# A feed-forward's first product by seven block products, with d_ff passed in two halves

## The chip, the core and the metric

The kernel runs on one core of one Trainium2 chip. The metric is the time of one execution on the device, in microseconds (us). Before the change it is 640.53 us, the median of three runs (640.45 to 642.44).

A core has TensorE (PE, matrix products into PSUM), VectorE (DVE), ScalarE (ACT), GpSimd (POOL), and SyncE (SP), whose queue here issues all transfers between memory and the on-chip buffers.

## The reference

Attention for 4 batches, 8 heads, 768 positions and 64 columns per head, then a feed-forward block on its output. Cut to what matters:

```python
k_sum = k.reshape(B, H, nb, 32, D).max(axis=3)     # nb = 24 blocks of 32 positions
v_sum = v.reshape(B, H, nb, 32, D).mean(axis=3)
scores_l = where(|i - j| < 16, scale * q @ k.T, -1e9)
scores_s = scale * q @ k_sum.T + log(32)
a = softmax(concatenate([scores_l, scores_s]))
x = a @ concatenate([v, v_sum])                    # 3072 tokens of 512 columns
h = x @ w_in                                       # 512 x 2048
g = maximum(h, 0) + log1p(exp(-abs(h)))            # softplus
out = g @ w_out                                    # 2048 x 512
```

The weights come as float64, the rest as float32.

## The kernel before

**Groups and phases.** The 3072 tokens are 12 chunks of 256, three to a batch. Chunks are joined into groups of tokens (line 301): [0, 1], [2], [3, 4], [5, 6], [7, 8], [9, 10], [11]; five hold 512 tokens and two hold 256. The 2048 columns of d_ff are 16 tiles f of 128. The phases (lines 303 and 304) are: group 0 with f 0 to 10, group 1 with f 0 to 10, then both with f 11 to 15, then each further group with all 16. The attention of a group must be done before its phase; it is spread over the phases ahead.

**Attention of a unit** (`attention`, line 557; two heads' pairs of one chunk). TensorE makes scores `sc` (L582), VectorE scales and masks them and takes maxima (L595), ScalarE takes exponentials (L603), VectorE inverts the sums, POOL or VectorE normalizes (L616), VectorE transposes 32x32 squares (L642), which go through memory to finish the transposition (L650, L654), and TensorE multiplies by the value windows (`xo`, L673). The first group uses TensorE for the transposition instead. The block means of v and maxima of k are made once per batch (`Sums`); for the first batch v's come from six matmuls over six loads of 128 positions (`declare_first_values`, L403).

**Precision.** Each operand a of the feed-forward is split into a rounded part and the remainder, ah + al, and each product is three matmuls: ah*bh, ah*bl, al*bh. ScalarE makes `xh` from `xo` (L689), VectorE makes `xl` (L693).

**Weights** (`weights`, line 702). Each tile f is one 512 KB load from w_in (L722) and one from w_out (L719) as 64-bit words. Integer work on VectorE (L735 to L750), ScalarE (L756) and POOL (L764) turns them into two float32 parts (L768, L775). All 16 tiles stay on the chip.

**Feed-forward** (`feed_forward`, line 785). For each f: the first product goes into `ph`, 128 x 512 fp32, in 12 matmuls (L804: four blocks of d_model by three terms); ScalarE takes softplus twice, rounded into `gh` (L824) and exact in place (L828); VectorE takes the difference `gl` (L832); 12 matmuls of the second product add into four `po` tiles (L841). PSUM has eight buffers of 2 KB per partition: four `po`, two for `sc`, and two that `ph` and `xo` share in turn.

```python
ph()[:, :n_x], lhsT=w1()[:, i1, part, cc * P:(cc + 1) * P], rhs=a()[:, cc, :n_x],
start=cc == 0 and i == 0, stop=cc == NCC - 1 and i == 2,
```

**The order of work.** Every piece of work is a task with an engine (or a choice of engines), a declared cost, and the buffers it reads and writes. Tasks are numbered in the order in which the program declares them. The text `SEQUENCE` lists these numbers; a letter takes the second or third choice of engine. `Order.issue` (line 122) runs the tasks' code in that order, so it is the order of each engine's queue, and also the order in which two uses of one buffer follow each other. Engines run their queues in order and wait for each other by semaphores.

Of the kernel before, what the change touches and what calls it, by code (L numbers as in the profile page):

```python
# [75 lines left out]
class Order:  # L76
# [45 lines left out]
    def issue(self, sequence):  # L122

        begun = set()
        for word in sequence.split():
            task = self.tasks[int(word.rstrip("ab"))]
            assert all(other in begun for other, _ in task.after) and task not in begun
            begun.add(task)
            task.ways[" ab".index(word[-1]) if word[-1] in "ab" else 0].run()
        assert len(begun) == len(self.tasks)  # L130
# [17 lines left out]
0 2 64 3 43 4 45 5 68 6 133 7 160 8 51 1 9 47 132 10 44 11 49 12 13 46 14 55 15 72 96 53 16 134a 138a 17 73 151  # L148
161a 74 162 100 84 135 163 142 164 136 137 57 18 165 85 139 19 59 20 166 52 48 86 61 75 76a 65 388 50 70 77 167
21 396a 168 104 66 78 140a 156 141a 147 79 105 69 54 189 143a 56 152a 144 87 58 106 190 153 88a 60 62 145 154  # L150
146 22 116 63 155 80 71 107 157 23 117 24 67 25 26 97 27 148 158 28 169 29 118 30 170 31 108a 32 101 33 34 98 35
149a 99 36 159 37 38 103 39 150 40 102 119 191a 120a 81 179 195 192 89 91 193 90 180 41 92 194 82 93 128 171a 83
196 130 42 94 109 131 111 95 110 199 112 172 309 391 175 173 129 174 197 200 113 389 176 392 121 114 387 123 122
115 390 124 397 198 177 125 178 318 126 181a 219 127 220 185 182 239 310 183 240 201a 184 319 311 202 186 399
312 320 414 313 269 205 325 209 203 187 204 413 321 188 225 416 314 415 326 206 322 315 417 327 400 316 210 221a
317 270 323 207a 208 229 401 324 222 331 223 230 224 289 245 402 403a 329 241a 328 226 422a 332 404 337 405 242
227 279 243 249 333 228 330 338 339 425 244 395 211a 335 334 246 340 215 343 212 235 406 213 247 214 336 344 248
341 426 216 584 345 393 342 250 601 347 346 427 602 217a 604 407 218 348 585 588 349 394 398 231a 408 428 409
290 232 355 350 603 233 234 351 589 236 353 356 352 357 586 605 358 410 429a 237 354 418 255 238 280 359 419
610a 430 420 251a 423 361 587a 431 259 295 252 590 421 253 613 362 254 360 614 256 363 432 365 411 434 424 412  # L160
615 433 257a 367 258 364 594 435 591a 373 368 616 598 617 299 366 369 374 370 371 375 595a 436 376 592 627 599a
372 437 606 628 377 629 380 438 381 378 439 382 593 383 271 631 379 440 441 445 285 442 272 451 273 446 275 274
443 447 596 452 600 444 630 448 276 453 612 449 454 618 260 457 300 619 277a 463 608 458 597 278a 459 450 464
460 455 636a 465 466 456 384 261 461 385 462 265 262 386 469 263 264 639 470 471 472 475 266 654 640 620 611 481
476 477 607 305 478 609 467 291 655 658a 653 468 482 267a 473 483 641 292 474 293 479 484 480 294 487 268 493
296 488 661 485 489 676 494 490 623 495 486 642 622 297 643a 491 621 675 281a 499 496 298a 677 644 492 508 680a
282 500 283 284 501 497 509 502 286 510 498 662 301a 516 511 287a 663 288 683 512 302 804 645 503 303 805 513
304 807 517 806 504 803 664 522 306 505a 812a 506a 518 507 519 665a 307 514 528 666 523 308a 524 525 667 684 515
534 542 529 546 530 685 531 624 815 646 648 520 647 649 686 632 687a 635 521 634 535 688 633 526 637 816 638 536
625 527 689 830 838a 626 817 532 829 537 650 550 668 671 656 533 651 670 551 669 652 538 659 539 543 657 540 552  # L170
818 660 553 541 819a 833 556 831 832 544 548 554 545 557 558 555 559 672 562 673 690 678 674 682 841 563 564 693
# [3 lines left out]
862a 723 865 716 724 725 721 726 860 729 869 881a 866 884 730 731 826 885 722 870 827 834 899 828 886 727 836  # L175
732 901 848 863 728 840 735 850 851 839 887 837 898 741 736 902 835 900 849 737 738 733 742 888a 743 864 734 744
747 907 889 910 748 749 852 750 871 739 877 853 911 890 879 753 854 912 759 891 883 892 754 882 913 914a 740 894
# [3 lines left out]
1042 788 926 793 933 927 794 934 797a 795 798 1043 796 799 928 800a 801 1044 929 935 802 938 930 939 931 940  # L181
1045 1060 941 1046 1047 936 1061 1048 937 1062 942 943 1049 1063 944 1055 1050 1064a 1074 1075 1083a 1051 1077
1065 1076 1078 950 945 1056 1066 1058 946 1059 947 948 951 952 953 1086 956 1087 1067 1068 1069 1088 1070 962
949 957 954 1089 1090a 1091 958 955 963 960 959 1092 964 1100 965 1101 1109a 961 1071 968 1072 1079 1081 1073
1093 1094 1095 1096 974 969 1080 1082 970 1084 971 1085 980 975 1103 1102 976 1104 977 1097 966 1105 1098 1107
1099 1106 1108 1112 981 1110 982 1111 967 1113 1232 972 1236 983 1114 973 978 979 984 1115 1116a 1117 985 986
1233 1118 1237 1234 1238 992 987 1119 1120 988 1121 989 990 993 1122 994 995 998 1235a 1239a 1242 1004 999 1000
1246 1001 1249 1250 1258 1251 1010 1005 1253 1006 1252 1243 991 996 1007 1247 1240 1016 1011 1012 1244 1248 1241
1261 997 1262 1002 1013 1263 1245 1003 1008 1009 1017 1014 1264 1265a 1266 1018 1015 1123 1019 1267 1275 1276
1284 1020 1124 1277 1021 1024 1125 1279 1278 1022 1025 1254 1023 1027 1026 1126 1028a 1268 1269 1270 1271 1029  # L190
1255 1134 1127 1257 1128 1256 1259 1129 1260 1287 1135 1136 1130 1288 1131 1132 1137 1289 1133 1138 1272 1139
1280 1281 1273 1290 1140 1283 1291a 1282 1285 1274 1286 1292 1146 1141 1293 1302 1306 1303 1142 1301 1143 1144
1147 1148 1149 1152 1294 1295 1296 1297 1158 1153 1154 1155 1298 1159 1160 1309 1304 1299 1305 1300 1145 1307
1310 1150 1308 1161 1311 1151 1156 1157 1162 1312 1313a 1163 1314 1164 1315 1324 1328 1325 1323 1170 1165 1316
1166 1317 1167 1168 1318 1171 1319 1172 1173 1176 1320 1177 1178 1331 1326 1321 1179 1327 1322 1169 1329 1332
1174 1330 1333 1175 1180 1181 1182 1334 1335a 1336 1188 1183 1337 1184 1185 1186 1189 1190 1191 1194 1338 1339
# [5 lines left out]
1463 1394 1477 1464 1478 1486a 1401 1480 1479 1465 1481 1399 1400 1402 1407 1466 1467a 1468 1403 1405 1404 1408  # L202
1469 1409 1410 1406 1413 1470 1471 1472 1411 1414 1473 1415 1416 1412 1419 1474 1420 1421 1489 1482 1475 1422
1484 1476 1417 1483 1485 1490 1487 1418 1488 1491 1425 1423 1426 1492 1493a 1424 1431 1494 1427 1428 1495 1429
# [10 lines left out]
def kernel(  # L215
# [731 lines left out]
    for f in range(NF):  # L947
        weights(f)
# [44 lines left out]
```

## Time and profile before

| what | before |
|---|---|
| median of the runs | 640.53 us |
| the profiled execution: its span, first to last instruction | 638.3 us |
| granted clock of TensorE, mean | 0.991 |
| TensorE busy, matmuls | 623.1 us (98%) |
| VectorE / ScalarE / POOL busy | 277.6 / 316.3 / 75.6 us |
| moved by DMA | 86.51 MB, 136 GB/s over the span |
| first product L804 | 960 matmuls of 512 columns and 384 of 256 |
| second product L841 | 1152 matmuls of 512 columns |

The profiled execution's own time is its span and about what lies between that and the median, 2.2 us. Each row of a view names the line, the engine, the operation, what it writes and reads ("gl<-ph,gh"), and a count. "Idle before" is the time that the engine stood before this work, with what ended the wait. In the list of groups a matmul's mean covers its way through the array, and matmuls overlap; what one costs in a stream is read from the chain, where each piece lasts until the next begins.

### The profile page before, as it was taken

What the parts mean: (1) busy time and instruction counts of PE and PEld (TensorE: products, weight loads), DVE (VectorE), ACT (ScalarE), POOL (GpSimd) and SP (SyncE); (2) the same over time, 40 slices, a digit from 0 to 9 for tenths busy, and PEclk for the clock granted to TensorE, in tenths of its full rate; (3) what the DMA queues carried; (4) which work ended last, traced back from release to release, by engine and by line L of the source; (5) the groups of instructions that cost most, each with busy time, mean ns of one, the idle gap of its engine ahead of it and who ended that gap; (6) DMA issues with size and microseconds to landing.
All of it is one profiled execution on the core that took longest, in us unless ns stands there. A gap on an engine that the chain in (4) does not pass through costs nothing.

```text
span 638.3 us, 11177 instructions
## 1 busy us (share of the span) xinstructions
PE 623.1 (98%) x4284; PEld 505.5 (79%) x4284; DVE 277.6 (43%) x753; ACT 316.3 (50%) x762; POOL 75.6 (12%) x70
## 2 busy tenths in 40 slices
PE   7889999999999999999999999999999999999997
PEld 6576777888888888887777877787888888888996
DVE  5879988779643435213451445432411111341111
ACT  4879887479652555215472434462522222552222
POOL 3333322334201130001000030000000000000000
PEclk9889999999999999999999999999999999999999
DMA  9999699744668742141354653453300400311100
GB/s 291 247 262 324 234 224 248 218 139 117 210 201 243 222 139 88 63 134 42 137 167 116 179 143 106 130 145 107 98 1 0 139 1 0 109 57 60 48 1 34
DMA packets 86629, 86.51 MB, mean 136 GB/s; under 512 B 26704, under 2 KB 72368, under 8 KB 86576
## 3 DMA queue, kind: packets, MB, share of 16 engines
q1 hardware_dynamic: 86576, 85.80, 46.2%
q8 instruction: 34, 0.56, 0.3%
q14 instruction: 19, 0.16, 0.1%
HBM read 65.01 MB, written 18.35 MB: 131 GB/s over the span
## 4 chain that ended last, share of the span: by engine, by line
PE 91%; DMA 3%; ACT 3%; SPq 1%; DVE 1%; issue 0%; ACTq 0%
PE po L841 42%; PE ph L804 41%; PE xo L673 4%; PE sc L582 3%; DMA raw<-w_out_dram 2%; DMA k<-kT_dram 1%; ACT sp L603 1%; PE vt L403 1%; DVE sp L616 1%; ACT t L738 0%; SPq L722 0%; ACT pT L633 0%; PE pt L629 0%; ACT raw L756 0%; ACT w L768 0%
## 5 line engine op out<-in xcount | busy, mean ns | idle before, releaser
L804 PE MATMUL ph<-xh,w 128*128 128x512 f32 (+1 forms) x896 | 261.7, 365 | 4.0 <-DVE gl L832 2.5
L841 PE MATMUL po<-w,gh 128*128 128x512 f32 x768 | 204.8, 396 | 0.0
L804 PEld LDWEIGHTS ph<-xh,w 128*128 128x128 f32 x896 | 161.8, 189 | 35.0 <-DVE gl L832 3.1
L832 DVE TENSOR_TENSOR gl<-ph,gh 128x512 fp32r<-128x512 f32 (+1 forms) x112 | 68.2, 611 | 232.5 <-ACT ph L828 211.2
L841 PEld LDWEIGHTS po<-w,gh 128*128 128x128 f32 x768 | 142.3, 188 | 32.7 <-issue 0.8
L804 PE MATMUL ph<-xl,w 128*128 128x512 f32 (+1 forms) x448 | 163.0, 364 | 0.5 <-DVE xl L693 0.5
L824 ACT ACTIVATE gh<-ph 128x512 fp32r<-128x512 f32 (+1 forms) x112 | 60.2, 538 | 207.3 <-PE ph L804 169.3
L841 PE MATMUL po<-w,gl 128*128 128x512 f32 x384 | 115.6, 398 | 0.0
L804 PEld LDWEIGHTS ph<-xl,w 128*128 128x128 f32 x448 | 84.6, 189 | 16.2 <-DVE xl L693 1.3
L841 PEld LDWEIGHTS po<-w,gl 128*128 128x128 f32 x384 | 71.0, 188 | 17.1 <-issue 0.9
L603 ACT ACTIVATE sp<-sp,nm 128x120 f32<-128x120 f32 x192 | 73.1, 382 | 4.4 <-DVE nm L595 4.1
L828 ACT ACTIVATE ph<-ph 128x512 f32<-128x512 f32 (+1 forms) x112 | 59.4, 531 | 0.0
L764 POOL TENSOR_TENSOR t<-t,raw 128x1024 int32<-128x1024 int32 (+1 forms) x18 | 41.8, 2328 | 91.7 <-DVE t L750 26.3
L595 DVE CUSTOM_DVE_ANT_0 sp<-sc,added 128x120 f32<-128x120 f32 x192 | 40.7, 277 | 17.7 <-PE sc L582 17.3
L824 ACT ACT_TABLE_LOAD x24 | 30.8, 1283 | 34.0 <-PE ph L804 30.7
L693 DVE TENSOR_TENSOR xl<-xo,xh 128x512 fp32r<-128x512 f32 x24 | 16.5, 689 | 46.2 <-ACT xh L689 46.2
L603 ACT ACTIVATION_READ_ACCUMULATOR sp<-sp,nm 128x1 f32 x192 | 35.9, 187 | 0.0
L689 ACT CAST xh<-xo 128x512 fp32r<-128x512 f32 x24 | 14.1, 586 | 40.9 <-PE xo L673 40.9
L616 DVE TENSOR_TENSOR sp<-sp,ss 128x960 f32<-128x960 f32 x21 | 26.4, 1258 | 0.5
L673 PEld LDWEIGHTS xo<-pT,v 120*64 120x64 f32 x640 | 20.3, 138 | 7.5 <-issue 6.2
L642 DVE STREAM_TRANSPOSE tb<-sp 128x1024 f32<-128x1024 f32 x20 | 24.8, 1240 | 1.5 <-POOL sp L616 1.2
L353 POOL TENSOR_TENSOR st<-st 96x512 f32<-96x512 f32 (+1 forms) x10 | 10.1, 1011 | 127.9 <-DMA st<-v_hp_dram 127.5
(60 smaller groups left out, 379.4 us busy)
## 6 DMA issues: line engine op xcount, KB each, us to landing
squares<-tb SPq DMA_DIRECT2D x20, 512.0 KB
pT<-squares SPq DMA_DIRECT2D x80, 128.0 KB
raw<-w_in_dram SPq DMA_DIRECT2D x16, 512.0 KB
raw<-w_out_dram SPq DMA_DIRECT2D x16, 512.0 KB
kf<-kT_dram SPq DMA_DIRECT2D x16, 384.0 KB
out_dram<-ob SPq DMA_DIRECT2D x11, 512.0 KB
q<-qT_dram SPq DMA_DIRECT2D x20, 256.0 KB
st<-v_hp_dram SPq DMA_DIRECT2D x12, 384.0 KB
```

Source lines behind the costliest of these rows:

```text
L582: nc.tensor.matmul(unit(g * NU + h * NPAIR + i)[r * QW:(r + 1) * QW, k0:k1], lhsT=q[rows, w * QW:(w + 1) * QW], rhs=k[rows], start=True, s ...
L595: nc.vector.tensor_tensor_reduce(out=sp()[:, n], in0=unit(n), in1=added()[:, kinds.index((lows[w], lows[w + 1]))], scale=-SCALE, scalar=FL ...
L603: nc.scalar.activation(sp()[:, n], sp()[:, n], AF.Exp, bias=nm()[:, n:n + 1], scale=-1.0, accum_out=ss()[:, n:n + 1],)
L616: engine.tensor_tensor(sp(), sp(), s, op=ALU.mult)
L642: nc.vector.transpose(out=tb().rearrange("p k (u q) -> p u k q", q=SQ), in_=tiles.sp().rearrange("p u (k q) -> p u k q", q=SQ),)
L673: nc.tensor.matmul(xo()[h * D:(h + 1) * D, g * CH + w * QW:g * CH + (w + 1) * QW], lhsT=tiles.v(g)[:, w, h * D:(h + 1) * D], rhs=queries(g ...
L764: nc.gpsimd.tensor_tensor(a, a, word(0, I32), op=ALU.add)
L804: nc.tensor.matmul(ph()[:, :n_x], lhsT=w1()[:, i1, part, cc * P:(cc + 1) * P], rhs=a()[:, cc, :n_x], start=cc == 0 and i == 0, stop=cc == ...
L824: nc.scalar.activation(gh()[:, :n_x], ph()[:, :n_x], AF.Softplus)
L828: nc.scalar.activation(ph()[:, :n_x], ph()[:, :n_x], AF.Softplus)
L832: nc.vector.tensor_sub(out=gl()[:, :n_x], in0=ph()[:, :n_x], in1=gh()[:, :n_x].bitcast(F32),)
L841: nc.tensor.matmul(po[t](), lhsT=a()[:, t * P:(t + 1) * P], rhs=w2()[:, i2, part], start=f == f0 and i == 0, stop=f == f1 - 1 and i == 2,)
```

## The change

**Groups and phases.** Six groups of 512 tokens. d_ff is passed in two halves of eight tiles: groups 0 to 4 with the first half, group 5 with all 16, then groups 4, 3, 2, 1, 0 with the second half. The second half's weights are loaded into the buffers of the first half while group 5 is in work (`arrive`). The partial outputs of groups 0 to 4 go to memory and come back, and so does the attention's output x of these groups (`keep`, `attended`). All attention, twenty units after the first four, stands ahead of group 5's phase.

**First product.** For groups 0 and 1 in the first half it stays: 12 matmuls of 512 columns per tile, on xh and xl. Everywhere else two tiles of d_ff are taken together (`hidden_pair`): the product of a 2 x 2 block of weights (128 columns of d_ff and 256 rows of d_model each) with a 2 x 2 block of x (256 rows, 256 tokens) is made of seven block products in place of eight. Each is six matmuls of 256 columns. The products are called by their weight operand: a11, a12, a22 are blocks, s1 to s4 are sums of blocks. They go into halves of two PSUM buffers, `hx` (called z: a11, s2, a12, s4) and `hy` (called y: s3, s1, a22), each of the size of one `ph`, and are combined by a copy p1 and seven VectorE operations of 256 columns: u2, u3, u4 into on-chip buffers, y1, z0, z1, y0 in place. z and y then hold the two tiles. The sums of weights are made once per pair (`sums_of_weights`: joined, combined, and split in two parts), those of x once per group and half (`prepare`: three differences of x blocks more, seven splits in place of four).

**Sums of v.** For the first batch, two loads of 128 positions in place of six; the rest is summed from the value windows that the attention loads anyway, in forty matmuls of 128 columns, one group of ten for each of four pairs of heads.

**Weights.** w_in and w_out are prepared by pairs of tiles, 1024 columns each, w_in by one load of 1 MB; the first pair of each half goes tile by tile.

The numbers of `SEQUENCE` are all new (2346 tasks). In a pair the numbers follow the declarations in `hidden_pair`: with a11 as 2232, p1 is 2233, s3 2234, s2 2235, u2 2236, u3 2237, s1 2238, u4 2239, y1 2240, a12 2241, z0 2242, s4 2243, z1 2244, a22 2245, y0 2246. The lines below hold the first pair of the second half for group 1 (from 2098) and for group 0 (from 2232).

```diff
 SEQUENCE = """
...
+2097a 1941 2048 2053 2056 2057 2218 2049 2061 2058 2062 2072 2063 2088 2068 2098 2099a 2101 2102 2100 2109 2103 2104
...
+2144 2230 2182 2187 2221a 2228a 2185 2148 2190 2191 2149 2183 2189 2192 2222 2168 2071 2231a 2225 2195 2196 2197 2232
+2235 2238 2233 2236 2241 2234 2242 2239 2237 2243 2245 2169 2173 2244 2246 2247 2174 2240 2248 2254 2249 2255 2256
...
-    groups = [[0, 1], [2]] + [[c, c + 1] for c in range(3, len(chunks) - 1, 2)] + [[len(chunks) - 1]]
-    SPLIT = NF // 2
-    phases = [(0, 0, 11), (1, 0, 11), (0, 11, NF), (1, 11, NF)]
-    phases += [(x, 0, NF) for x in range(2, len(groups))]
...
+    groups = [[c, c + 1] for c in range(0, len(chunks), 2)]
+    NX = len(groups)
+    HALF = NF // 2
+    phases = [(x, 0, HALF) for x in range(NX - 1)] + [(NX - 1, 0, NF)]
+    phases += [(x, HALF, NF) for x in reversed(range(NX - 1))]
+    BLOCKS = (0, 1, 2, 3)
+    WHOLE = 2
...
+            parts = {}
+            for i in range(n0, S // P):
+                parts[i] = buffer([P, DM], F32, "vn0", tag="gh", bufs=NU)
...
+            def sum_first(hp, windows, v_keys):
+                def sum_v():
+                    terms = [(ones()[:, NB - 4 * i:2 * NB - 4 * i], part()[:, hp * P:(hp + 1) * P]) for i, part in parts.items()]
+                    for w in range(n0 * P // QW):
+                        rows, of = (KW, shifted) if w else (QW, ones)
+                        terms.append((of()[:rows, NB - 2 * w:2 * NB - 2 * w], windows()[:rows, w]))
+                    for n, (of, values) in enumerate(terms):
+                        nc.tensor.matmul(
+                            total()[KW:KS, hp * P:(hp + 1) * P], lhsT=of, rhs=values,
+                            start=n == 0, stop=n == len(terms) - 1,
+                        )
+                order.add(PE, 2.2, sum_v, [*parts.values(), *v_keys, ones, shifted], [(total, hp)])
...
+        if x:
+            r = block(2 * i + hp // NG)
+            def take(copy):
+                copy(out=r(), in_=xo())
+            order.add(
+                ACT, act(NG * CH, True), lambda: take(nc.scalar.copy), [xo], [r],
+                ways=[Way(DVE, dve(NG * CH), lambda: take(nc.vector.tensor_copy))],
+            )
+            return r
...
+    def keep(x, n, r, held=None):
+        order.add(
+            SP, 0, lambda: nc.sync.dma_start(out=kept(x, n)(), in_=r()), held or [r], [kept(x, n)], size=256 * KiB, row=2048,
+        )
...
+    def prepare(x, n, r):
+        r11, r21, r12, r22 = (r.get(k) for k in range(4))
+        if n == 0:
+            split(r11, *operand(x, 0), NG * CH)
+        elif n == 1:
+            split(r21, *operand(x, 1), NG * CH)
+        elif n == 2:
+            less(r12, r11, r11)
+            split(r11, *operand(x, 2), NG * CH)
+        else:
+            split(r22, *operand(x, 3), NG * CH)
+            less(r22, r12, r12)
+            split(r12, *operand(x, 5), NG * CH)
+            less(r22, r11, r11)
+            split(r11, *operand(x, 4), NG * CH)
+            less(r11, r21, r21)
+            split(r21, *operand(x, 6), NG * CH)
...
+        tiles = [(out_of, i) for i in range(2) for out_of in range(2)] if apart else [(0, None), (1, None)]
+        for outer, which in tiles:
+            fs = [which] if apart else [0, 1]
+            n = len(fs) * DM
+            tag = f"{'wo' if outer else 'wi'}{g}" + (f"_{which}" if apart else "")
...
+                        src = w_in[pair].bitcast(U32)
+                        if apart:
+                            src = w_in[pair, :, :, which * P:(which + 1) * P].bitcast(U32)
...
+        def combined(engine):
+            a11, a12, a21, a22 = (a()[:, i, j] for i in range(2) for j in range(2))
+            engine.tensor_tensor(a22, a21, a22, op=ALU.add)
+            engine.tensor_tensor(a21, a11, a21, op=ALU.subtract)
+            engine.tensor_tensor(a11, a22, a11, op=ALU.subtract)
+            engine.tensor_tensor(a12, a12, a11, op=ALU.subtract)
...
+    TERMS = ((0, 0), (0, 1), (1, 0))
...
+    def hidden_pair(x, f):
+        (w0, of_0), (w1, of_1) = of_w(f), of_w(f + 1)
+        sw = s_bufs[f]
+        y, z = bank([P, 2, CH], "hy"), bank([P, 2, CH], "hx")
+        p1, u2, u3, u4 = (buffer([P, CH], F32, name, bufs=1) for name in ("p1", "u2", "u3", "u4"))
+        def of_s(k):
+            return lambda part, cc: sw()[:, part, k, cc * P:(cc + 1) * P]
+        left = {
+            "a11": (of_0, w0), "a12": (lambda part, cc: of_0(part, NG + cc), w0), "a22": (lambda part, cc: of_1(part, NG + cc), w1),
+            "s2": (of_s(0), sw), "s4": (of_s(1), sw), "s3": (of_s(2), sw), "s1": (of_s(3), sw),
+        }
+        def product(a, n, to, half):
+            lhs, held = left[a]
+            of_x, (buf,) = operand(x, n)
+            def run():
+                y(), z()
+                for cc in range(NG):
+                    for m, (wa, xa) in enumerate(TERMS):
+                        nc.tensor.matmul(
+                            to()[:, half], lhsT=lhs(wa, cc), rhs=of_x(xa)[:, cc * CH:(cc + 1) * CH],
+                            start=cc == 0 and m == 0, stop=cc == NG - 1 and m == 2,
+                        )
+            return order.add(
+                PE, 0.72, run, [(held, 0), (held, 1), (buf, 0), (buf, 1), (y, "whole"), (z, "whole")], [(to, half)],
+            )
+        def combine(out, a, b, op, reads, write):
+            order.add(
+                DVE, dve(CH), lambda: nc.vector.tensor_tensor(out(), a(), b(), op=op), reads, [write],
+            )
+        def half(t, n):
+            return lambda: t()[:, n]
+        begins = product("a11", 0, z, 0)
+        begins.after += [(order.writer[operand(x, n)[1][0], 1], False) for n in range(7)]
+        first_after(begins)
+        order.add(
+            ACT, act(CH, True), lambda: nc.scalar.copy(out=p1(), in_=z()[:, 0]), [(z, 0)], [p1],
+            ways=[Way(DVE, dve(CH), lambda: nc.vector.tensor_copy(out=p1(), in_=z()[:, 0]))],
+        )
+        product("s3", 5, y, 0)
+        product("s2", 4, z, 1)
+        combine(u2, half(z, 1), p1, ALU.add, [(z, 1), p1], u2)
+        combine(u3, half(y, 0), u2, ALU.add, [(y, 0), u2], u3)
+        product("s1", 2, y, 1)
+        combine(u4, half(y, 1), u2, ALU.add, [(y, 1), u2], u4)
+        combine(half(y, 1), half(y, 1), u3, ALU.add, [u3], (y, 1))
+        product("a12", 1, z, 0)
+        combine(half(z, 0), half(z, 0), p1, ALU.add, [p1], (z, 0))
+        product("s4", 3, z, 1)
+        combine(half(z, 1), half(z, 1), u4, ALU.add, [u4], (z, 1))
+        product("a22", 6, y, 0)
+        combine(half(y, 0), u3, half(y, 0), ALU.subtract, [u3], (y, 0))
+        return [z, y]
...
+        pairs = x >= WHOLE or f0 > 0
+            if f0 == 0 and f == HALF:
+                arrive(range(HALF, NF))
+            if not pairs:
+                hs, n = hidden(x, f), 0
+            elif f % 2 == 0:
+                hs, n = hidden_pair(x, f), 0
+            else:
+                n = 1
...
+    def attended(x):
+        r = {}
+        x_bufs.pop(x, None)
+        for n in BLOCKS:
+            order.group = f"a{x}.{n // 2}.{n % 2 * NG}"
+            r[n] = block(n)
+            def load(n=n):
+                nc.sync.dma_start(out=r[n](), in_=kept(x, n)())
+            order.add(SP, 0, load, [kept(x, n)], [r[n]], size=256 * KiB, row=2048)
+            prepare(x, n, r)
+    def arrive(fs):
+        for f in fs[::2]:
+            weights(f // 2)
+        for f in fs[::2]:
+            sums_of_weights(f)
...
+        if x == NX - 1:
+            sums = attend(x, sums)
+        elif x and not f0:
+            sums = attend(x, sums)
+        elif f0:
+            attended(x)
```

More of the change, by code (lines that the diff above doesn't have):

```diff
@@ L485, in load_v @@
                         )
-                    order.add(SP, 0, load_v, [], [self.v_keys[-1]], size=48 * KiB * n, row=512, begin=begin)
+                    order.add(SP, 0, load_v, [], [self.v_keys[-1]], size=48 * KiB * n, row=512)
             def k_sums(copy):
@@ L694, in attention @@
-        order.add(DVE, dve(NG * CH), low, [xo, (xh, c, hp)], [(xl, c, hp)], due=due_x)
-    w_bufs = {}
-    def weights(f):
-        order.group = f"w{f}"
-        for i0, i1 in [(0, 1), (1, 2)] if f < 2 else [(0, 2)]:
-            n = (i1 - i0) * DM
-            tag = f"w{f}_{i0}" if f < 2 else f"w{f}"
+        order.add(PE, 1.2, values, [pT, *((pT, k) for k in range(NSQ)), *tiles.v_keys], [xo])
+        if x:
[7 more added lines that the diff above has]
+            return r
@@ new lines, in attention, with of_x, of_bank, high @@
+        xw = whole_x(x)
+        for g in range(NG):
+            key = xw[hp + g]
+            def of_x(part, key=key):
+                return key[0]()[:, key[1], part, cols]
+            def of_bank(g=g):
+                return xo()[:, g * CH:(g + 1) * CH]
+            def high(of_x=of_x, of_bank=of_bank):
+                nc.scalar.copy(out=of_x(0), in_=of_bank())
+            order.add(ACT, act(CH, True), high, [xo], [(*key, 0, i)])
+            def low(of_x=of_x, of_bank=of_bank):
+                nc.vector.tensor_sub(out=of_x(1), in0=of_bank(), in1=of_x(0).bitcast(F32))
+            order.add(DVE, dve(CH), low, [xo, (*key, 0, i)], [(*key, 1, i)])
@@ L809, in feed_forward @@
-            parts = [range(0, NG), range(NG, NCC)] if x == 0 and f < 2 else [range(NCC)]
-            for ccs in parts:
-                def product_of(ccs=ccs, product=product):
-                    product(ccs)
-                task = order.add(
-                    PE, 0.35 * size * len(ccs), product_of,
-                    [(a, c, hp) for a in (xh, xl) for c in groups[x] for hp in range(0, NHP, NG) if hp in ccs]
-                    + [(w1, i) for i in range(2)],
-                    [ph], due=when, after=[last] if last and ccs[0] == 0 else [],
-                )
-                if ccs[0] == 0:
-                    last = task
@@ L835, in feed_forward @@
-            order.add(DVE, dve(n_x), rest, [ph, gh], [gl])
+            if not pairs:
[4 more added lines that the diff above has]
+                n = 1
+            order.group = f"f{x}.{f}"
+            h = hs[n]
+            halves = [(h, 0), (h, 1)] if pairs else [h]
+            w2, i2, _ = w_out_of[f]
+            gh = buffer([P, CT], F32R, "gh", bufs=4)
+            gl = buffer([P, CT], F32R, "gl", bufs=4)
@@ L837, in project @@
+            order.add(DVE, dve(CT), rest, [*halves, gh], [gl])
             def project(tokens, which, f=f, w2=w2, i2=i2, gh=gh, gl=gl):
@@ L867, in reload @@
                     nc.sync.dma_start(out=ob(), in_=partial[x, i]())
-                order.add(SP, 0, reload, [partial[x, i]], [(ob, 0), (ob, 1)], size=512 * KiB, row=2048, after=[last])
+                order.add(
+                    SP, 0, reload, [partial[x, i]], [(ob, 0), (ob, 1)], size=512 * KiB, row=2048, after=[products[-1]],
+                )
             for t in range(2):
@@ L893, in leave @@
                         nc.sync.dma_start(out=out[r0:r0 + P, :], in_=ob()[:, t])
-                    order.add(SP, 0, leave, [(ob, t)], [], size=256 * KiB, row=2048, due=end + 4)
+                    order.add(SP, 0, leave, [(ob, t)], [], size=256 * KiB, row=2048)
             else:
@@ L947 @@
-    for f in range(NF):
-        weights(f)
+        r = {}
+        for i in range(len(groups[x])):
+            for hp in range(0, NHP, NG):
+                c = groups[x][i]
+                if chunks[c][1] == 0 and hp == 0:
+                    sums = Sums(chunks[c][0])
+                    sums.declare()
+                order.group = f"a{x}.{i}.{hp}"
+                n = 2 * i + hp // NG
+                r[n] = attention(x, i, hp, Places(c, hp, sums, pads), False)
+                if x < NX - 1:
+                    keep(x, n, r[n])
+                if x < WHOLE:
+                    prepare_whole(x, n, r)
+                else:
+                    prepare(x, n, r)
```

524 lines of the change are left out of this document (345 added, 179 removed), and 19 rows, old and new, of the table SEQUENCE.

## The prediction

> **What bounds the kernel now.** I read the page's busy times and slices first, then the time by stages, then the chain that ended last.
>
> ```profile
> span 638.3 us, 11177 instructions
> ...
> PE 623.1 (98%) x4284; PEld 505.5 (79%) x4284; DVE 277.6 (43%) x753; ACT 316.3 (50%) x762; POOL 75.6 (12%) x70
> ...
> PE   7889999999999999999999999999999999999997
> ```
>
> ```profile
> 0.00:100.00 100.00, 88.49 (x814) 68.43 (x818) 79.14 (x192) 78.91 (x173) 32.52 (x39) 0.95 0.94 264
> 100.00:635.00 535.00, 534.65 (x3480) 437.09 (x3472) 198.44 (x562) 237.12 (x590) 43.06 (x31) 1.00 0.38 111
> ```
>
> The columns are PE, PEld, DVE, ACT and POOL, then granted clock, DMA share, GB/s. From 100 us to the last matmul TensorE is busy 534.65 us of 535, at a granted clock of 1.00, with VectorE at 198, ScalarE at 237 and DMA at 0.38. In the first 100 us every resource is crowded: DMA 0.94, VectorE and ScalarE 79, TensorE 88 with waits. So after 100 us a microsecond of matmul removed is a microsecond of span, and a gap put between matmuls is one too. The chain shows the price of a matmul.
>
> ```profile
> 520.54 2.78 PE ph L804 x12
> 523.33 2.78 PE po L841 x12
> ...
> 630.43 1.43 PE ph L804 x12
> 631.87 2.80 PE po L841 x12
> ```
>
> Twelve matmuls of 512 columns take 2.78 to 2.80 us (0.2325 each), and the 256-column ones of the last, half-sized group 1.43 or 1.44 (0.1195 each). A matmul's time goes with its columns, and two halves cost only 2.8% over a whole. That also settles whether the new, narrower products would be held up by their weight loads: the half group loads new weights for each 256-column matmul already.
>
> **The first product.** A pair of hidden tiles took 2 x 2.79 = 5.58 us for 512 tokens. Seven block products of six 256-column matmuls are 42 x 0.1195 = 5.02. Forty pairs go this way (the first two groups keep the plain product for the first half of d_ff): 40 x 0.56 = 22.4 us off. The two half-sized groups disappear as well: 32 products at 1.435 become halves of full ones at 1.395, another 1.3. Together -23.7. The second product and the attention's matmuls stay as they are.
>
> **The sums of v.**
>
> ```profile
> 22.59 4.77 PE vt L403 x10
> ```
>
> Six sums over 512 columns run as twelve instructions of 0.477 us, 5.7 us. Now forty sums of 128 columns run as eighty, at a quarter each 9.5 us: +3.8, all in the start where TensorE waits on others anyway, so between 0 and 3.8; I take 3.8. Four loads of 256 KB go: at the 264 GB/s above 4 us of transfers, which I leave in the bounds of the start below.
>
> **The block products' hand-overs.** This is the term that decides. Each pair writes into two buffers, hx and hy, of 2 x 256 fp32 columns, each the size of one ph. hx takes a11, s2, a12, s4 and hy takes s3, s1, a22. Between them one copy and seven VectorE operations read and rewrite halves of these buffers: p1 and u2 read hx, u3 and u4 read hy, and so on. Before, ph passes as a whole: all matmuls, then all readers, then the next matmuls, with a second ph to hide it. What a passing costs is seen here.
>
> ```profile
> 67.79 0.68 DVE L832 TENSOR_TENSOR gl<-ph,gh 128x512 fp32r<-128x512 f32 x1
> ...
> 68.52 0.50 PE L804 MATMUL ph<-xh,w 128*128 128x512 f32 x1 [1.26 <-DVE gl L832]
> ...
> 68.86 0.39 PE L804 MATMUL ph<-xl,w 128*128 128x512 f32 x1
> ```
>
> ```profile
> 631.58 0.29 PE L804 MATMUL ph<-xh,w 128*128 128x256 f32 x1
> ...
> 631.96 0.39 ACT L824 ACTIVATE gh<-ph 128x256 fp32r<-128x256 f32 x1 [2.16 <-PE ph L804]
> 632.24 0.38 ACT L828 ACTIVATE ph<-ph 128x256 f32<-128x256 f32 x1
> ...
> 632.66 0.42 DVE L832 TENSOR_TENSOR gl<-ph,gh 128x256 fp32r<-128x256 f32 x1 [2.40 <-ACT ph L828]
> ```
>
> The last 256-column matmul starts at 631.58, its slot ends at 631.70, the reader starts at 631.96: 0.26 us. A reader of 256 columns takes 0.39 on ScalarE, 0.42 on VectorE, and one reader follows another after 0.04 (632.62 to 632.66). Back to TensorE: the read ends at 68.47, the matmul starts at 68.52, and its successor is 0.34 later instead of 0.23, so 0.16. A product that must wait for one fresh read of its buffer stands still for 0.26 + 0.42 + 0.16 = 0.84 us, unless a product into the other buffer fills the time.
>
> Does a product into one half wait for a reader of the other half? No row of before shows it, since no buffer there is read while the rest is still being written. The ends are no wait, and the wait for the whole buffer. I take the whole buffer, which is how every ph in the trace changes hands. [...]
>
> I walked the order of words with these prices. The first pair of group 1's second half begins 2098 2099a 2101, which is a11, p1, s2: hx, its reader, hx, with nothing of hy between. It stands bare for 0.84. The first pair of group 0's second half, 2232 2235 2238 2233 2236 2241 2234 2242 2239 2237 2243 2245 is a11, s2, s1, p1, u2, a12, s3, z0, u4, u3, s4, a22. s2 ends at 1.43, p1 (ScalarE) runs 1.69 to 2.08, u2 2.12 to 2.54, a12 may start at 2.70 where s1 ended at 2.15: 0.55. s4 waits 0.13 for z0. s3 ends at 4.13, u4 and u3 end at 5.15, a22 starts at 5.31 against 4.98: 0.33. Sum 1.01 us, against the 0.56 that the pair saves. Over the forty pairs, with the other words of VectorE and ScalarE in their places, it comes to 49 us, from 0.1 to 3.6 a pair (the dear ones have p1 or u2 behind a softplus or a mask). If passing cost nothing and only the readers' own time counted, it would be 26. So 0 to 49, and I take 49: the durations are measured, and only the rule that a half waits for the other is assumed.
>
> The readers themselves, about 3.4 us per pair, fit: VectorE has 337 us free after 100 us, and the forty pairs ask 134.
>
> **The start: when group 1's first product can begin.**
>
> ```profile
> 3.43 7.42 DMA raw<-w_out_dram
> ```
>
> ```profile
> 64.42 2.43 POOL L764 TENSOR_TENSOR t<-t,raw 128x1024 int32<-128x1024 int32 x1 [4.80 <-DVE ss L610]
> ...
> 64.55 3.32 DVE L616 TENSOR_TENSOR sp<-sp,ss 128x960 f32<-128x960 f32 x1
> ```
>
> ```profile
> L616 DVE TENSOR_TENSOR sp<-sp,ss 128x960 f32<-128x960 f32 x21 | 26.4, 1258 | 0.5
> ...
> L750 DVE SCALAR_TENSOR_TENSOR t<-raw,t 128x1024 uint32<-128x1024 uint32 x14 | 17.1, 1225 | 0.4
> ...
> L742 DVE TENSOR_SCALAR t<-t 128x1024 f32<-128x1024 f32 x14 | 10.2, 728 | 2.0 <-ACT t L738 2.0
> L746 DVE TENSOR_SCALAR t<-t 128x1024 uint32<-128x1024 uint32 x14 | 10.1, 722 | 0.5
> ```
>
> Group 1 is now two chunks, and it comes after eight tiles of d_ff instead of eleven, so all its attention stands ahead of it. POOL and VectorE exclude each other here: the multiply that takes 1.258 us on average took 3.32 when it began 0.13 after a POOL add of 2.43. So I add both engines' SBUF work in the words ahead of group 1's first product. POOL: 8,192 columns of weight adds, six normalizations of 960 and about 10,000 columns of low parts and other sums, 24,000 columns at 2.43 per 1,024, 57 us. VectorE: eight times 0.728 + 0.722 + 1.225 = 21 us for the weights' integer steps and, estimated at the same rates, 29 for low parts, casts, magnitudes, normalizations and sums of v, 50 us. The first weights land at 10.85, so 107 us of exclusive work end at 118 at best. Before had done 200 of the two products' matmuls at 100 us; the change needs 192, three more value units (3 us), nearly four more score units (4 us) and the 3.8 above: 109 if TensorE fares as before. So the start loses 9 us. Filled only as VectorE was on average (79 of 100 us) it would end at 146 and lose 37; it loses 0 if work ahead in the order can run later than it stands. I take 12, nearer the low end, as the two engines take turns.
>
> **The rest.**
>
> ```profile
> q1 hardware_dynamic: 86576, 85.80, 46.2%
> ```
>
> ```profile
> SPq L483 <- PE xo L673: 73.5, 15, 10.8
> ```
>
> The x blocks of five groups go to memory and back, and the partial outputs of five groups instead of two: some 18 MB more. At the 111 GB/s for a share of 0.38 that is 62 us of the full DMA, on top of 0.462 x 638 = 295. All attention now comes in the first half; without the second half's weights, the final stores and half of the 18 MB, about 275 us of DMA fall into some 335 us. It is hidden, so 0, but a late load is in the range. The second half's weights are prepared during the last group, with about 94 us of POOL and VectorE work that exclude each other where TensorE has 88 (78 of matmuls, about 10 of hand-overs): between 0 and 15, I take 3. The stores of x wait on SP for their copy, with the next unit's loads queued behind; SP waited 73.5 us in such a place before, for xo, and TensorE lost nothing: 0. The tail stays: four token tiles instead of two, stored one by one.
>
> **Sum.** The profiled span is 638.3, the median of the runs 640.5, so 2.2 lie around it. 640.5 - 23.7 + 3.8 + 12 + 49 + 3 = 684.6, say 685. A measurement of this kernel tells 0.3% (2 us) from no change.
>
> **Rivals.** First, the halves are independent, or the hand-overs are covered: 685 - 49 = 636, and with a start that costs nothing 624. It is the other side: faster from the point where a pair loses less than about 0.1 us, that is 0.56 less the 17.5 us of the other terms over forty pairs. For it: the order names hx and hy by halves in the writes it declares. Against it: ph's whole-buffer turns above. Second, the second half's weights come late and the last group waits for them: +15 in place of 3, 697. For it: 94 against 88. Against it: the loads can begin when the last group leaves each tile. Third, the hand-overs cost the readers' time alone, 26: 662, in the low end of my own range.
>
> **How the numbers follow.** Forecast 0.63 with the third rival in it, own range 655 to 702; first rival 0.25; second 0.12. 630 to 706 leaves out about half of the first rival and the upper half of the second. Faster 0.22 and same 0.03 are the first rival; slower 0.75 is the rest.
>
> **What would show it.** Right: idle ahead of the block products' matmuls, released by VectorE or ScalarE readers of hx and hy, near 1.2 us per pair; TensorE below 95% busy in the last 200 us, with VectorE below half. Block products at 0.72 us each. Group 1's first product near 121 us. Wrong: TensorE gapless in the last phases, a pair at 5.0 us.

## The result, and the profile after

The changed kernel takes 754.6 us (median of four runs, 748.9 to 757.4) against 640.5 (640.0 to 642.4) for the kernel before, run beside it: a ratio of 1.177, 95% interval 1.172 to 1.183. The prediction was 685, range 630 to 706. The sign was right; the size was 70 us short, outside the range.

First the page of the changed kernel: span, busy times, the slices of three engines and of the clock, and the chain that ended last.

```profile
span 755.4 us, 13144 instructions
...
PE 648.5 (86%) x4880; PEld 548.8 (73%) x4880; DVE 497.4 (66%) x1130; ACT 323.0 (43%) x800; POOL 252.9 (33%) x213
...
PE   8887779979698899979979877788899899789998
...
DVE  7689899646766746766758987874735455445542
...
POOL 5366556325632230141245734460500602201000
PEclk9798898989899989989999998999999999999999
...
PE 55%; DVE 27%; DMA 7%; ACT 3%; SPq 3%; issue 3%; POOL 2%; DVEq 0%; ACTq 0%; POOLq 0%
```

TensorE fell from 98% busy to 86%; VectorE rose from 277.6 us to 497.4 and POOL from 75.6 to 252.9. VectorE now carries 27% of the chain. The time by stages shows where (columns as in the prediction: window, length, PE, PEld, DVE, ACT, POOL, granted clock, DMA share, GB/s):

```profile
0.00:100.00 100.00, 82.51 (x867) 66.22 (x868) 82.04 (x213) 57.53 (x175) 53.68 (x60) 0.88 0.78 234
100.00:200.00 100.00, 80.69 (x683) 63.50 (x685) 71.39 (x194) 61.35 (x179) 51.90 (x48) 0.90 0.81 222
200.00:300.00 100.00, 91.46 (x826) 78.71 (x827) 64.93 (x198) 52.22 (x146) 27.42 (x26) 0.94 0.65 185
300.00:400.00 100.00, 85.47 (x740) 72.54 (x739) 69.66 (x173) 47.38 (x125) 26.71 (x19) 0.97 0.56 165
400.00:500.00 100.00, 79.74 (x444) 69.11 (x442) 85.03 (x121) 46.85 (x67) 52.77 (x33) 0.91 0.24 84
...
600.00:700.00 100.00, 90.63 (x539) 79.45 (x539) 49.18 (x94) 23.89 (x46) 13.29 (x10) 0.98 0.14 45
700.00:755.00 55.00, 49.94 (x279) 42.57 (x277) 22.21 (x44) 9.45 (x18) 0.00 (x0) 0.99 0.16 58
```

Two different losses can be read here. After 600 us TensorE has gaps while VectorE is half idle: that is the hand-overs' pattern. From 100 to 200 and from 300 to 500 us TensorE is idle more, and at 400 to 500 VectorE is at 85 and POOL at 53 of 100: there VectorE itself is short of time. What TensorE waited for from 40 us on (engine and line, releaser, us in total, times, longest):

```profile
PE hx L1095 <- DVE u L1105: 15.0, 14, 4.2
PE hy L1095 <- DVE u L1105: 12.0, 7, 5.3
PE hx L1095 <- DVE gl L1165: 11.3, 6, 4.1
PE sc L653 <- DMA q<-qT_dram: 7.0, 2, 4.8
PE hx L1095 <- DVE hx L1105: 6.8, 9, 1.4
```

The combining (L1105) is the largest releaser, but not the only one. I also took every matmul's start from the trace. Uninterrupted block products follow at 0.119 us a matmul, second products at 0.2324. With these as the nominal, the stretch from the first product at 44.0 us to the last matmul holds 512 us of products, 55 of attention on TensorE, 114 of gaps, and 26 of extra time in slow matmuls: 7 in 69 single ones that come first after a wait (0.10 each), 19 in runs of matmuls that follow each other at about 1.8 times the nominal (0.213 us for 0.119, 0.427 for 0.2324).

### The profile page after: what moved, and what is told of

Read it like the earlier page. It is cut to its first block, busy times and chain, and to the rows that moved or that the text cites. A ratio compares the mean times of both kernels' runs of the same rounds, so it can differ in the third digit from the quotient of the medians.

```text
span 755.4 us, 13144 instructions
## 1 busy us (share of the span) xinstructions
PE 648.5 (86%) x4880; PEld 548.8 (73%) x4880; DVE 497.4 (66%) x1130; ACT 323.0 (43%) x800; POOL 252.9 (33%) x213
## 4 chain that ended last, share of the span: by engine, by line
PE 55%; DVE 27%; DMA 7%; ACT 3%; SPq 3%; issue 3%; POOL 2%; DVEq 0%; ACTq 0%; POOLq 0%
PE po L1172 22%; PE hx L1095 15%; PE hy L1095 10%; DVE u L1105 2%; PE xo L751 2%; DVE x L813 2%; PE sc L653 2%; DVE x L806 2%; DVE t L936 2%; DMA kf<-kT_dram 2%; DVE hx L1105 2%; DVE t L944 2%; PE vt L452 2%; DVE w L969 1%; SPq L732 1%
## 5 line engine op out<-in xcount | busy, mean ns | idle before, releaser
L813 POOL TENSOR_TENSOR x<-r,x 128x512 fp32r<-128x512 f32 x37 | 52.1, 1416 | 188.2 <-ACT x L806 120.8
L1095 PE MATMUL hx<-x,sw 128*128 128x256 f32 x480 | 81.0, 307 | 25.0 <-DVE u L1105 6.5
L1095 PE MATMUL hx<-x,w 128*128 128x256 f32 x480 | 74.1, 291 | 24.4 <-DVE gl L1165 11.3
L1095 PEld LDWEIGHTS hx<-x,sw 128*128 128x128 f32 x480 | 68.9, 205 | 32.1 <-DVE u L1105 7.7
L1095 PEld LDWEIGHTS hx<-x,w 128*128 128x128 f32 x480 | 65.7, 192 | 33.6 <-DVE gl L1165 13.9
L1095 PE MATMUL hy<-x,sw 128*128 128x256 f32 x480 | 71.7, 294 | 9.9 <-DVE u L1105 9.4
L1095 PEld LDWEIGHTS hy<-x,sw 128*128 128x128 f32 x480 | 65.5, 201 | 11.5 <-DVE u L1105 10.6
L1055 PE MATMUL ph<-xw,w 128*128 128x512 f32 x192 | 50.6, 414 | 6.3 <-DVE gl L1165 3.3
L1105 DVE TENSOR_TENSOR u<-hx,p 128x256 f32<-128x256 f32 x40 | 16.9, 423 | 51.6 <-PE hx L1095 33.7
L1105 DVE TENSOR_TENSOR u<-hy,u 128x256 f32<-128x256 f32 x80 | 32.0, 420 | 27.6 <-PE hy L1095 26.7
L1055 PEld LDWEIGHTS ph<-xw,w 128*128 128x128 f32 x192 | 37.4, 199 | 17.4 <-DVE gl L1165 4.1
L1095 PE MATMUL hy<-x,w 128*128 128x256 f32 x240 | 38.4, 298 | 5.2 <-DVE u L1105 2.6
L1095 PEld LDWEIGHTS hy<-x,w 128*128 128x128 f32 x240 | 33.6, 200 | 8.4 <-DVE hy L1105 4.1
```

The source lines that it names most:

```text
L813: engine.tensor_tensor(to(1), a(), to(0).bitcast(F32), op=ALU.subtract)
L1055: nc.tensor.matmul(ph(), lhsT=lhs(part, cc), rhs=xw[cc][0]()[:, xw[cc][1], a], start=cc == 0 and n == 0, stop=cc == NCC - 1 and n == 2,)
L1095: nc.tensor.matmul(to()[:, half], lhsT=lhs(wa, cc), rhs=of_x(xa)[:, cc * CH:(cc + 1) * CH], start=cc == 0 and m == 0, stop=cc == NG - 1 an ...
L1105: DVE, dve(CH), lambda: nc.vector.tensor_tensor(out(), a(), b(), op=op), reads, [write],
```

## The experiments

Line numbers shift by a few lines between the kernels: L1095 of the change is L1094 to L1107 elsewhere.

**1. The combining left out.**

```diff
-                DVE, dve(CH), lambda: nc.vector.tensor_tensor(out(), a(), b(), op=op), reads, [write],
+                DVE, dve(CH), lambda: None, reads, [write],
```

(and the copy p1 likewise)

> The eight copies and sums between the block products of a pair (p1, u2, u3, u4, y1, z0, z1, y0) are left out, so the hidden values are wrong; products, softplus, operands and the order stay. In the trace after, counted from the first product at 44.0 us to the last matmul, TensorE has 512 us of product slots, 55 of attention, 114 of gaps and 26 of slots at about 1.84 times their time. Theory (hand-overs of hx and hy, 49 in the prediction, make most of it): 625 to 660, and the gaps that stay are softplus ones. Rival (VectorE and POOL are late with the operands of the next group, the weights and the masks, whatever the hand-overs): 690 to 720, as VectorE gets 134 us back but the waits at the phases' beginnings stay.

695.9 us (690.9 to 698.9; ratio 1.087, 1.082 to 1.092). That is the rival's range. The combining costs 58.7, and what is left is 55 above the kernel before. In its last five phases TensorE waited only once for a product's buffer, 2.8 us in all (window 466 to 695, columns as in the waits above):

```profile
PE hx L1095 <- DVE gl L1165: 2.8, 1, 2.8
```

**2. Each half in a bank of its own, last five phases.**

```diff
+            ys = [bank([P, CT], "hy"), bank([P, CT], "hy")]
+            zs = [buffer([P, 2, DM], F32, "hx", "sc", 1, psum)] * 2
```

> In the last five phases (groups 4 to 0, second half of d_ff) each half of hx and hy lies in a PSUM bank of its own; the order and every operation stay, but the softplus of hy runs in two pieces. Theory (a half waits for the readers of the other half, because they share a bank): the 29 us of gaps and 7 us of stretched slots of these phases go down to below 10, so about 725. Rival (TensorE waits for the values it needs, or for the readers' own time): no change, 750 to 757.

749.1 us (744.5 to 750.5). The theory's 725 is missed by far, and the result lies just under the rival's range. The interval of the ratio, 1.165 to 1.173, overlaps that of the change, so the total alone settles little more. The waits do. First the change, at the first pair of group 4's second half:

```profile
498.65 0.87 PE L1095 MATMUL hx<-x,w 128*128 128x256 f32 x6
...
499.63 0.42 DVE L1105 TENSOR_TENSOR u<-hx,p 128x256 f32<-128x256 f32 x1 [0.90 <-PE hx L1095]
500.09 0.42 DVE L1105 TENSOR_TENSOR u<-hy,u 128x256 f32<-128x256 f32 x1
...
500.57 0.98 PE L1095 MATMUL hy<-x,sw 128*128 128x256 f32 x6 [1.05 <-DVE u L1105]
```

Then the same products with the halves apart:

```profile
496.61 0.88 PE L1107 MATMUL hx<-x,w 128*128 128x256 f32 x6
...
497.32 0.87 PE L1107 MATMUL hy<-x,sw 128*128 128x256 f32 x6
...
497.93 0.41 DVE L1117 TENSOR_TENSOR u<-hx,p 128x256 f32<-128x256 f32 x1
...
498.38 0.42 DVE L1117 TENSOR_TENSOR u<-hy,u 128x256 f32<-128x256 f32 x1
498.39 0.99 PE L1107 MATMUL hx<-x,sw 128*128 128x256 f32 x6 [0.20 <-DVE u L1117]
```

In the change s1 (500.57) goes into the second half of hy and starts 0.06 us after u3's read of the first half has ended (500.51); with the halves apart it follows a12 at once, ahead of u3. So a half does wait for a reader of the other half here. But over the five phases keeping the halves apart takes the gaps only from 29 to 23 us: most hand-overs wait for a reader of their own half, which banks can't change. (The softplus of hy runs in two pieces here, 0.66 us together against 0.60, which is not separated from the rest.)

**3. Only the order inside a pair.** In the last twenty pairs. The first pair of group 0's second half:

```diff
-2232 2235 2238 2233 2236 2241 2234 2242 2239 2237 2243 2245 2169 2173 2244 2246 2247 2174 2240
+2232 2235 2238 2233 2236 2234 2241 2239 2237 2240 2243 2169 2245 2173 2242 2244 2247 2174 2246
```

that is a11 s2 s1 p1 u2 s3 a12 u4 u3 y1 s4, a second product (2169), a22, z0 z1 y0, in place of a11 s2 s1 p1 u2 a12 s3 z0 u4 u3 s4 a22, then z1, y0 and y1 with words of second products between them.

> Only the order of words changes, in the 20 pairs of the last five phases: a11 s2, then p1 u2 while s1 s3 go into hy, then a12 s4 into hx while u4 u3 y1 read hy, then a22. Theory (whole-bank turns): a pair's loss falls from 1.3 to about 0.4 us, so about 735 to 740. Rival (turns by halves, or a cost that does not depend on the order): 750 to 757 or slower.

730.6 us (728.9 to 732.4; ratio 1.142, 1.139 to 1.144). That is 24 us from the order of words alone, 1.2 a pair, a little more than the theory expected. It shows that the order matters. That the turns are by bank it does not show, since this order also leaves more time between a reader and the next product into the same half (a second product stands ahead of a22).

**4. POOL's share on VectorE.**

```diff
-788 812 604a 761 613
+788 812 604 761a 613
```

(the letter picks the engine; the same for every word of POOL that has the choice)

> Only letters change: the 115 words of POOL that have a choice (low parts, differences, normalizations, sums of the weights, of v) go to VectorE; POOL keeps the weights' integer adds. VectorE gets some 85 us of work. Theory that POOL and VectorE exclude each other and stretch each other's operations (45 us or more on VectorE in the trace after): faster by 10 to 40 us, 715 to 745. Rival (VectorE's own load is the bound of groups 2 to 5): slower, 770 to 800.

747.8 us (744.1 to 750.2; ratio 1.168, 1.164 to 1.173), which is neither the theory nor the rival. In the profiled runs group 1's first matmul comes at 119.7 us in place of 129.0, but its second then waits 5.58 us for a low part of x that VectorE makes. Group 2's pairs begin 6.7 us earlier than in the change (191.4 against 198.1), and the lead stays between 6 and 10 us to the end.

**5. The order by bank in all forty pairs.** The edit is that of the third experiment.

> The order by bank of the third experiment (730.6 us) now in all forty pairs. Theory (the order inside a pair sets its loss everywhere): another 0.8 to 1.0 us for each of the twenty pairs of groups 2 to 5, so 711 to 717. Rival (in these phases the readers come late because VectorE's queue is full, whatever the order): 726 to 732.

725.8 us (721.8 to 728.3), at the edge of the rival's range. By the medians only 5 us come from the twenty pairs of groups 2 to 5, where the theory had 16 to 20. (Between the two profiled runs the stretch from group 2's first pair to the end of group 5 shrinks by 10, from 301 to 291 us.) The readers still come late there: between 185 and 490 us TensorE waits 12.8 us for `u` with a product into hx, against 12.1 in the change.

**6. No operand work**, on top of the first experiment.

```diff
-            DVE, dve(n), lambda: low(nc.vector), [a, (*key, 0)], [(*key, 1)], port=True,
+            DVE, dve(n), lambda: None, [a, (*key, 0)], [(*key, 1)], port=True,
```

(and the differences in `less`; the products read the rounded part twice)

> On top of the first experiment (no combining, 695.9 us): the differences of the x blocks and the low parts of the seven operands are left out for groups 2 to 5 and for all second halves (some 80 us of POOL and 29 of VectorE); the products use the rounded part twice. Theory (the operands of a group are late at its first pair): the gaps at the beginnings of groups 2, 3, 4, 5 and of the second half of group 3 go, 12 to 20 us of gaps and 3 to 5 of stretched slots: 671 to 681. Rival (the attention and its transfers are late): 690 to 697.

674.3 us (670.8 to 675.0), which is 21.6 off, as the theory had it. The waits for x from 180 us on, which were 11.1 us in the first experiment, are gone.

**7. No second weights**, on top of that.

```diff
+                order.skip = True
                 arrive(range(HALF, NF))
+                order.skip = False
```

> On top of the experiment without operand work: the second half's weights and their sums are neither loaded nor prepared, the second half multiplies with the first half's. Theory (they are late for group 5, as 'the second half's weights' in the prediction, 0 to 15 us): the 14 us of gaps and stretched slots of group 5 go, 12 to 16 us off. Rival (group 5 waits for softplus or for partial sums): within 3 us.

655.6 us (654.8 to 660.9), which is 18.7 off: the theory, somewhat more than its size. From 340 us on TensorE is now busy 314.09 of 315 us: a half phase of eight tiles takes 42.2 us, as worked out (4 x 5.02 + 8 x 2.79 = 42.4). The stretch in which the second half's weights would be made, before and after they are left out (window, length, PE, PEld, DVE, ACT, POOL, clock, DMA share, GB/s):

```profile
390.00:445.00 55.00, 44.19 (x250) 39.02 (x249) 47.42 (x49) 30.89 (x40) 29.22 (x14) 0.91 0.22 81
```

```profile
390.00:445.00 55.00, 55.00 (x341) 49.32 (x340) 8.54 (x13) 15.19 (x29) 0.00 (x0) 1.00 0.06 20
```

In the first, all of TensorE's waits, 10.8 us in four, are for `gl`, the softplus remainder that VectorE makes, and VectorE is busy 47.42 of 55 us, against 8.54 without the weights.

**8. No stores of x blocks and partial outputs**, on top of that.

```diff
-            SP, 0, lambda: nc.sync.dma_start(out=kept(x, n)(), in_=r()), held or [r], [kept(x, n)], size=256 * KiB, row=2048,
+            SP, 0, lambda: None, held or [r], [kept(x, n)], size=256 * KiB, row=2048,
```

(the same for the partial outputs; both are reloaded from an input of the same size)

> On top of the experiment without second weights: the x blocks and the partial outputs are not stored to memory (10 MB less in the first half), and are reloaded from an input of the same size. Theory of the prediction (the added traffic is hidden): within 3 us. Rival (it holds up the loads of attention and SP's queue): 5 to 20 us off.

652.3 us (649.1 to 657.7), 3 us less and within the spread of the runs. The stores, 10.5 MB by the two pages (94.96 to 84.48), are hidden. The loads back are still made, so this does not test them.

**9. Order and VectorE together**: the edits of the fifth and the fourth experiment in one.

> The order by bank in all forty pairs (725.8 us) together with POOL's words on VectorE (747.8 alone, against 754.6). Theory (POOL is the slow link up to group 2's first product, and its share adds to the order's): 708 to 720. Rival (VectorE is the bound of groups 2 to 5, so that the readers come later still): 726 to 740.

714.5 us (708.6 to 715.6; ratio 1.113, 1.108 to 1.118), in the theory's range. It is the fastest version that keeps the change's whole work, and 74 us slower than the kernel before.

**10 and 11. The combining back on a VectorE with room**, in the change's order and in the order by bank. Both on top of experiment 7.

> The combining is back, in the order of the change, on top of the experiment without operand work and without second weights (655.6 us): VectorE has 95 us less to do than in the change. Theory (a pair's own order makes the loss, 0.7 to 1.2 us a pair): 683 to 703. Rival (the loss is the readers' place in a full queue of VectorE): 657 to 670.

> The same with the order by bank in all forty pairs. Theory (with this order and a free VectorE the readers hide behind the products of the other buffer, 0.36 us a pair at most): 656 to 670. Rival (seven products in two buffers cannot hide them in any order): 675 to 690.

695.7 us (695.0 to 697.4) and 664.2 (659.9 to 666.9): both the theory. The last 100 us in the change's order, then the last 95 in the order by bank:

```profile
590.00:690.00 100.00, 93.80 (x542) 80.94 (x540) 42.27 (x85) 21.03 (x40) 0.00 (x0) 1.00 0.14 47
```

```profile
565.00:660.00 95.00, 95.00 (x575) 84.58 (x574) 42.31 (x88) 21.74 (x42) 0.00 (x0) 1.00 0.13 45
```

VectorE does the same 42.3 us in both. In the second TensorE has no gap left. Together with experiments 1, 5 and 7 this gives the price of combining, in all and for each of forty pairs:

| | change's order | order by bank |
|---|---|---|
| VectorE with operands and second weights | 754.6 - 695.9 = 58.7 (1.5) | 725.8 - 695.9 = 29.9 (0.75) |
| without them | 695.7 - 655.6 = 40.1 (1.0) | 664.2 - 655.6 = 8.6 (0.2) |

**12. The start without POOL's share**, on top of experiment 7.

> On top of the experiment without combining, operand work and second weights (655.6 us, of which some 35 lie ahead of group 2's pairs): POOL's words go to VectorE, as in the fourth experiment. Theory (the start waits for POOL, and for VectorE's operations that POOL stretches): group 1's first product comes near 119 instead of 129 us and nothing gives it back, 640 to 648. Rival (the start waits for transfers and for the attention's chain of engines): 652 to 658.

657.1 us (655.0 to 657.4), the rival's number. But the wait is not the rival's. Group 1's first matmul moved from 128.9 to 121.7 us, and its second waits for `xw`, a low part of x that POOL made before and VectorE makes now:

```profile
121.66 0.50 PE L1066 MATMUL ph<-xw,w 128*128 128x512 f32 x1
128.24 1.22 PE L1066 MATMUL ph<-xw,w 128*128 128x512 f32 x2 [6.08 <-DVE xw L851]
```

So moving POOL's share to VectorE gains nothing, since the start then waits for VectorE.

## Why the prediction was short

- **The first product, -23.7: right as far as it can be seen.** Where nothing interrupts, eight tiles take 42.2 us against 16 x 2.79 = 44.6 before, and block products of six matmuls at 0.119 the 0.72 us of the prediction.
- **The hand-overs, +49: right in kind, and near in size, in part by luck.** The walk had 49, 1.2 a pair. With room on VectorE they measure 40 (experiments 7 and 10), as the change stands 58.7; the rest goes with the other work on VectorE. No row of before shows that a half waits for a reader of the other, which the walk took as given. Experiment 2 shows it (s1 starts 0.06 us after u3's read of the other half, and ahead of u3 with the halves apart), but the walk put 23 of its 49 on it (49 less the 26 of the third rival). Measured, it is 6 of 29 us in the last five phases, and the readers' own turns are the bulk. The first rival's premise, that independent halves would cost nothing, fell with this. (By the walk's own prices u4 of its worked pair can begin only at 4.13 + 0.26 = 4.39, which makes that pair's sum 1.13, not 1.01; it matters little.)
- **"The readers themselves fit: VectorE has 337 us free": the step that failed.** It compared forty pairs' 134 us with VectorE's idle time over the whole stretch, and left out that the seven operands of each group and half must be made as well, with four differences (not three, as the section on the change has it) and seven low parts in each of nine phases; after group 1 that work was in no term of the sum. The groups of the profile after show it:

```profile
L813 POOL TENSOR_TENSOR x<-r,x 128x512 fp32r<-128x512 f32 x37 | 52.1, 1416 | 188.2 <-ACT x L806 120.8 <-DVE x L806 59.0 <-DVE ss L681 8.3
L822 POOL TENSOR_TENSOR r<-r 128x512 f32<-128x512 f32 x22 | 30.9, 1409 | 75.8 <-DVE x L813 39.7 <-DVE r L821 16.5 <-ACT r L763 15.1
L813 DVE TENSOR_TENSOR x<-r,x 128x512 fp32r<-128x512 f32 x26 | 29.3, 1142 | 0.2
L806 DVE CAST x<-r 128x512 fp32r<-128x512 f32 x28 | 22.5, 811 | 5.5 <-PE hx L1095 5.3
L821 DVE TENSOR_TENSOR r<-r 128x512 f32<-128x512 f32 x14 | 13.0, 934 | 2.7 <-ACT r L763 1.8 <-DMA raw<-r 0.6
```

  These are 83 us of POOL and 65 of VectorE. A subtraction of 512 columns, 0.687 us before (L832, with one operand in PSUM), takes 1.14 here beside POOL's. In experiment 4, where POOL makes none of them, it takes 0.70, and a cast 0.42 in place of 0.81:

```profile
L812 DVE TENSOR_TENSOR x<-r,x 128x512 fp32r<-128x512 f32 x63 | 42.7, 704 | 2.7 <-ACT x L805 2.5
L820 DVE TENSOR_TENSOR r<-r 128x512 f32<-128x512 f32 x36 | 24.3, 685 | 4.2 <-DMA raw<-r 1.8 <-ACT r L762 1.8 <-DMA r<-raw 0.5
L805 DVE CAST x<-r 128x512 fp32r<-128x512 f32 x28 | 11.7, 422 | 4.8 <-PE hx L1094 4.6
```

  There all 99 subtractions and the casts take 78.7 us of VectorE. So the 59 that POOL did in 83 us saved VectorE only 14. The work is due when a group's first pairs are, and differences and low parts cost 21.6 us (experiment 6). One such place, the first pair of group 2:

```profile
192.02 2.35 DVE L813 TENSOR_TENSOR x<-r,x 128x512 fp32r<-128x512 f32 x2
192.25 1.58 POOL L813 TENSOR_TENSOR x<-r,x 128x512 fp32r<-128x512 f32 x1 [1.15 <-DVE x L806]
...
195.81 0.38 DVE L1105 TENSOR_TENSOR u<-hx,p 128x256 f32<-128x256 f32 x1
196.22 0.43 DVE L1105 TENSOR_TENSOR hx<-hx,p 128x256 f32<-128x256 f32 x1
...
196.57 0.41 DVE L1105 TENSOR_TENSOR u<-hy,u 128x256 f32<-128x256 f32 x1
...
197.03 1.23 PE L1095 MATMUL hy<-x,sw 128*128 128x256 f32 x4 [5.35 <-DVE u L1105]
```

  u2 and u3 stand behind the operands and other small work in VectorE's queue, the next product waits for u3, and TensorE stands 5.35 us. Two terms that were priced apart, hand-overs and operands, meet in one queue.
- **The second half's weights, +3 (0 to 15): too small.** They cost 18.7 (experiment 7). The second rival named the place, with 15. The 18.7 is measured with neither combining nor operand subtractions in the kernel, so it isn't their meeting. In the longest of the four waits (4.1 us) `gl` stands behind sums of weights in VectorE's queue; in two others (2.45 and 2.75) the softplus that it needs stands behind weights on ScalarE. The prediction compared 94 us of work with 88 of TensorE's, and left out the place of the softplus words in these queues.
- **The start, +12: too small.** I had group 1's first product at 121; it comes at 129.0. Between 40 and 130 us VectorE is busy 81.95 of 90, against 75.3 before, and ScalarE 53.5 against 71.0. What remains without combining, operand work, second weights and stores is 652.3, against 640.5 - 23.7 + 3.8 = 620.6: 32 us, most of it ahead of 200 us (from 200 to 630 us TensorE is busy 424.66 of 430 in experiment 8). There TensorE waits 23.6 us between 44 and 200 us, 14.4 of it ended by VectorE, 4.1 by transfers and 1.3 by ScalarE; before had 3.7 in this window. Which work on VectorE is the late one was not tested; moving POOL's share there doesn't help (experiment 12).
- **The rest, 0: right for the stores** (3 us, experiment 8). The loads back were not taken away.

Against the prediction's terms, the 70 us that it was short are 21.6 of operands, put at nothing, 19.7 of the start (31.7 for 12), 15.7 of the second weights (18.7 for 3), 9.7 of hand-overs (58.7 for 49) and 3.3 of stores. They add up by construction, as the start is what remains after the removals, and the split depends on their order: in the table, taking away operand work and second weights makes the combining cheaper by 19 us as well.

## What to carry to other kernels

Work that moves from a full TensorE to a half-idle engine must be placed by stage and by queue, not by its sum: list everything the change hands to that engine, the preparation of new operands too, and look at the stage where it falls due. Where products and readers take turns in a buffer, walk the order of words; it was worth 29 us in the whole change, and 31 without operand work and second weights, with the same instructions. Ask what an operation costs beside POOL's: 83 us of POOL's work took only 14 off VectorE here. A product saved on TensorE pays only if what it adds elsewhere can wait.

## What was not expected of the hardware

The granted clock. I reckoned with 1.00; its mean is 0.943, against 0.991 before. After the wait of 5.35 us above, at least the next 3.5 us ran at half the clock (the clock is the third column from the right; windows before, in and after the wait):

```profile
186.00:191.00 5.00, 4.51 (x28) 3.75 (x27) 4.93 (x5) 0.89 (x2) 4.77 (x5) 1.00 1.06 291
191.00:197.00 6.00, 0.69 (x5) 0.48 (x5) 5.88 (x10) 1.02 (x4) 4.61 (x6) 0.80 0.35 106
197.00:200.50 3.50, 3.46 (x24) 3.24 (x28) 0.92 (x3) 1.38 (x5) 3.34 (x4) 0.50 0.85 275
200.50:203.00 2.50, 2.50 (x37) 2.25 (x30) 1.83 (x4) 1.27 (x2) 1.98 (x3) 0.83 0.11 29
```

So a long gap cost a second time here: the runs at about 1.8 times the nominal spacing add 19 us to the 114 of gaps. The granted clock is 0.50 from 197.0 to 201.4 us and 1.00 from there to 206.0. A shorter wait did it too: before 648.2 us TensorE waited 2.51 us, and from 648.6 to 651.9 the clock was 0.50.

Shorter waits, as most hand-overs are (the longest of them 1.38 us), left no such run behind in the last five phases: the gaps sum to 29 us there and the runs to 2.4, and the two stretches at half the clock follow the only longer waits, of 4.12 and 2.51 us.
